# Hedgehog feed: keys and queries of a tile in one pair of banks, values in single banks, sums and turned features two tiles behind, maxima over both banks

## The chip, the cores and the metric

The kernel runs on one core of one Trainium2 chip. The metric is the device time of one execution in microseconds (us). Before the change it is 2536.88 us, the median of three runs (2536.19 to 2537.71).

The engines are named as in the profile: PE (TensorE, matmul; PEld is its weight load), DVE (VectorE), ACT (ScalarE), POOL (GpSimd) and SP (SyncE, which here issues DMAs). PSUM is the memory that PE writes to; this kernel uses it as three pairs of banks (pool `psS`, 1024 f32 a partition each) and two single banks (pool `ps1`, 512 f32 each).

## The reference

Four layers on 2048 tokens of width 512, 32 heads of width 16: softmax attention (A), Hedgehog linear attention (B), A, B. Each adds its output to x.

```python
x = x + _A_ref(_layernorm(x), A_wqkv, A_wo)
x = x + _B_ref(_layernorm(x), B_wqkv, B_w_phi, B_wo)
x = x + _A_ref(_layernorm(x), A_wqkv, A_wo)
x = x + _B_ref(_layernorm(x), B_wqkv, B_w_phi, B_wo)

# inside _B_ref, per head:
pq = q @ w_phi                      # the kernel folds w_phi into the weights of q and k
pk = k @ w_phi
phi_q = concat(softmax(pq), softmax(-pq))
phi_k = concat(softmax(pk), softmax(-pk))
kv, z = phi_k^T v, sum(phi_k)
o = (phi_q @ kv) / (phi_q @ z + 1e-6)
```

## The kernel before

The tokens are cut into 16 tiles of 128 and into four blocks `j` of four tiles. A layer of type A (`LayerA.attention`) walks 512 steps, one for each group of four heads, query block and key tile. In a step PE makes scores (L909), ACT takes two exponentials of 128x1024 (L912), and PE multiplies an earlier step's exponentials by the values (L923). Between these PE gets pieces of side work from a queue of generators (`pump`), by a credit per step. One kind of side work is `tail(j)` (L961): the last part of the output projection of block j (`o_block`, two halves of two tiles), the residual sum (L603), and the layer norm of that block for the next layer. `Norm.half` (L495) runs after each half: `stats` (mean, and an inverse root by three Newton steps on 128x2 numbers) and, after the first half, `scaled` for tiles 0 and 1. `Norm.steps` (L513) then turns the four tiles on PE (L476), splits each into two f16 parts (L484 or L486, and L489), and calls `scaled` for tiles 2 and 3.

Where these run depends on flags. In the attention `state["att"]` is true: `stats` uses DVE and leaves the bias `b` as None (L445 to L455), and `scaled`, finding no bias, uses DVE (L461). After the attention `att` is false: `stats` runs its Newton steps on POOL (L441 to L443) and makes `b`, and `scaled` uses ACT (L463). With `soon` the Newton steps go to DVE in either case, and a bias is made (L448). Tails 0 to 2 run inside the attention, tail 3 mostly behind it.

Behind each attention stands the feed of the next layer: `LayerB.feed(j)` for the 16 tiles. It is in a block in which PE, DVE, ACT and POOL each run their instructions in the order in which the program writes them. For a tile this order is, before the change:

- PE: 12 matmuls for the key features (`pk`), 12 for the query features (`pq`), eight transposes of the query features of the tile before (`turn`, into two single banks, with a copy by ACT each, L1207), 12 for the values (`pbv`), 24 small ones that add up keys by values of the tile before (`gather`, into `kvp`). `pk`, `pq` and `pbv` take a pair from `psS` each and use half of it; one of the three pairs is held by `kvp` through the whole feed.
- DVE and ACT: for the keys and then for the queries the largest and smallest feature of each head (L1155, L1156), two differences (L1158, L1159) and the exponential (L1160, `expo`); then the copy of the values (ACT, L1128).
- DVE: the sum of the keys' exponentials (L1166), its reciprocal (L1167), a factor (L1169); the low part of the values (L1123); then sum and reciprocal for the queries. POOL multiplies by the reciprocals (L1175), keys first.
- ACT copies the keys' features to f16 (L1181, `halves`), POOL makes their low part (L1182).
- `between(t)`: pieces of tail 3. In tiles 0 to 3 a part of the output projection each (with `half` after tiles 1 and 3), in tiles 5 to 8 one turned tile each (PE L476, ACT L486, DVE L489).

`psum1` hands out the two single banks in strict alternation when `att` is false; whoever gets one waits until its last user has released it. Tile 15 has its own branch: its key features are split between DVE and POOL, two turned tiles are left to `rest`, which then makes the heads.

Of the kernel before, what the change touches and what calls it, by code (L numbers as in the profile page):

```python
# [9 lines left out]
F32 = mybir.dt.float32  # L10
# [3 lines left out]
AF = mybir.ActivationFunctionType  # L14
ALU = mybir.AluOpType
AX = mybir.AxisListType

P = 128
S = 2048
D = 512  # L20
H = 32
DH = 16
NC4 = D // P
NJ = S // 512
NT = S // P
# [11 lines left out]
KS = 16384.0  # L37
# [13 lines left out]
def mha_hedgehog_stack(ctx, tc, x_in, a_wqkv, a_wo, b_wqkv, b_wphi, b_wo, out, shmin=SHMIN):  # L51
    nc = tc.nc
# [115 lines left out]
    con = {}  # L168
# [235 lines left out]
    class Norm:  # L404
        def __init__(self, xts, name):
            self.xts = xts
            self.xnT = big([P, 2, NC4, 512], F16, f"xnT{name}")
            self.xn, self.par = {}, {}

        def stats(self, t0, n, soon=False):  # L410
            run(self.stats_parts(t0, n, soon))
# [82 lines left out]

        def half(self, t2):  # L495

            self.stats(2 * t2, 2)
            if t2 == 0:
                self.scaled(0), self.scaled(1)

# [145 lines left out]
    class LayerA:  # L646
# [314 lines left out]
        def tail(self, j, ob):  # L961
            xts = []
            ln = Norm(xts, f"a{self.li}_{j}")
            yield from o_block(j, {3: ob}, self.wo, con["oA"], self.x_dst, self.x_dst, xts, ln.half, wide=False, cs=(3,))
            for _ in ln.steps():
                yield GAP
                self.cost = 3
            self.out.append(ln.xnT)
# [98 lines left out]
    class LayerB:  # L1067
# [3 lines left out]
        def begin(self):  # L1071
            self.wqk = stgp.tile([P, 2, 2, NC4, 512], F16, tag="stg", name="wbqk")
            nc.sync.dma_start(self.wqk, dBqk)
            self.wv = []
            for a in range(2):
                t = wp.tile([P, NC4, 512], F16, tag="w", name=f"wbv{a}")
                nc.sync.dma_start(t, dBv[a])
                self.wv.append(t)
            self.kvp = None
            self.latek = self.lateq = None  # L1080
            self.qT, self.obs = [], []

        def feed(self, j, xnT, between=lambda t: None):

            if self.kvp is None:
                self.kvp = psS.tile([P, 2, 512], F32, tag="S", name="kvp")
            qT = [big([P, 4, 512], F32, f"qT{j}_{i}") for i in range(2)]
            self.qT.append(qT)
            for t in range(4):
                tt = 4 * j + t  # L1090

                def project(dst, w, passes=(0, 1, 2)):
                    for i in passes:
                        a, b = PASSES[i]
                        for c in range(NC4):
                            nc.tensor.matmul(dst, xnT[:, a, c, t * P:(t + 1) * P], w(b, c),  # L1096
                                             start=(i == 0 and c == 0), stop=(i == 2 and c == NC4 - 1))

                vt = np_.tile([P, 2, H, 17], F16, tag="yn", name="vt", bufs=5)
                nc.gpsimd.memset(vt[:, 0, :, 16:17], 1.0)  # L1100
                nc.gpsimd.memset(vt[:, 1, :, 16:17], 0.0)
                bank = lambda name: psS.tile([P, 2, 512], F32, tag="S", name=name)[:, 0, :]
                last = tt == NT - 1
                pk = bank("pk")
                project(pk, lambda b, c: self.wqk[:, 1, b, c, :])
                if last:
                    f_k = self.expo(pk)
                    self.kvb = np_.tile([P, 8, 32], F32, tag="yn", name="kvb", bufs=5)
                    nc.gpsimd.memset(self.kvb, 0.0)
                else:  # L1110
                    pq = bank("pq")
                    project(pq, lambda b, c: self.wqk[:, 0, b, c, :])
                if self.lateq is not None and tt < NT - 2:
                    self.turn(*self.lateq)
                pv_ = bank("pbv")
                project(pv_, lambda b, c: self.wv[b][:, c, :])
                if self.latek is not None:
                    self.gather(*self.latek)
                if last:
                    pq = bank("pq")  # L1120
                    project(pq, lambda b, c: self.wqk[:, 0, b, c, :], (0, 1))
                pvh = pv_.rearrange("p (h d) -> p h d", d=DH)
                low = lambda: nc.vector.scalar_tensor_tensor(  # L1123
                    vt[:, 1, :, 0:16], pvh, 2.0 ** -8, vt[:, 0, :, 0:16], op0=ALU.mult, op1=ALU.subtract)
                if not last:
                    f_k = self.expo(pk)
                    f_q = self.expo(pq)
                nc.scalar.activation(vt[:, 0, :, 0:16], pvh, AF.Copy, scale=2.0 ** -8)  # L1128
                if last:
                    fk = self.share_split(f_k, low)  # L1130
                    self.turn(*self.todo)
                    self.gather(tt, fk, vt)
                    project(pq, lambda b, c: self.wqk[:, 0, b, c, :], (2,))
                    self.blocks()
                    self.todo = [self.lateq, (tt, self.expo(pq), qT)]
                    for q in self.todo:
                        self.share(q[1], 1.0)
                    return
                self.share(f_k, KS)
                low()  # L1140
                if tt == NT - 2:
                    self.todo = self.lateq
                    self.latek = (tt, self.halves(f_k), vt)
                else:
                    self.share(f_q, 1.0)
                    self.latek = (tt, self.halves(f_k), vt)
                self.lateq = (tt, f_q, qT)
                between(tt)

        def expo(self, ps):  # L1150

            pf = ps.rearrange("p (h f) -> p h f", f=DH)
            mx = sp.tile([P, H], F32, name="mx")
            mn = sp.tile([P, H], F32, name="mn")
            nc.vector.tensor_reduce(mx, pf, AX.X, ALU.max)  # L1155
            nc.vector.tensor_reduce(mn, pf, AX.X, ALU.min)  # L1156
            f = pp.tile([P, H, 2, DH], F32, tag="p", name="f")
            nc.vector.tensor_tensor(f[:, :, 0, :], pf, mx.unsqueeze(2).to_broadcast([P, H, DH]), ALU.subtract)  # L1158
            nc.vector.tensor_tensor(f[:, :, 1, :], mn.unsqueeze(2).to_broadcast([P, H, DH]), pf, ALU.subtract)  # L1159
            nc.scalar.activation(f, f, AF.Exp, scale=con["pB"])  # L1160
            return f

        def part_sums(self, f, r, factor):

            su = sp.tile([P, r.stop - r.start], F32, name="su", bufs=4)
            nc.vector.tensor_reduce(su, f[:, r, :], AX.X, ALU.add)  # L1166
            nc.vector.reciprocal(su, su)  # L1167
            if factor != 1.0:
# [3 lines left out]
        def share(self, f, factor):  # L1172

            f3 = f.rearrange("p h s f -> p (h s) f")
            nc.gpsimd.tensor_tensor(f3, f3, self.part_sums(f3, slice(0, 64), factor), ALU.mult)  # L1175

        def halves(self, f):

# [260 lines left out]
```

## Time and profile before

| what | value |
|---|---|
| median of three runs | 2536.88 us |
| the profiled execution: its time | 2541.1 us |
| the profiled execution: its span | 2539.3 us |
| TensorE clock granted, mean | 0.983 |
| DVE busy | 974.3 us (38%) |
| POOL busy | 383.6 us (15%) |

The span is the time from the first to the last instruction; the execution's own time is 1.8 us longer. The times in the profile count from the start of the span. The first attention ends at about 1037 us and its feed at about 1211 us; the second attention ends at about 2289 us and its feed at about 2462 us. An engine's busy time is the union of its instructions; idle time of an engine that nobody waits for costs nothing.

### The profile page before, as it was taken

What the parts mean: (1) busy time and instruction counts of PE and PEld (TensorE: products, weight loads), DVE (VectorE), ACT (ScalarE), POOL (GpSimd) and SP (SyncE); (2) the same over time, 40 slices, a digit from 0 to 9 for tenths busy, and PEclk for the clock granted to TensorE, in tenths of its full rate; (3) what the DMA queues carried; (4) which work ended last, traced back from release to release, by engine and by line L of the source; (5) the groups of instructions that cost most, each with busy time, mean ns of one, the idle gap of its engine ahead of it and who ended that gap; (6) DMA issues with size and microseconds to landing.
All of it is one profiled execution on the core that took longest, in us unless ns stands there. A gap on an engine that the chain in (4) does not pass through costs nothing.

```text
span 2539.3 us, 51475 instructions
## 1 busy us (share of the span) xinstructions
PE 2433.9 (96%) x21346; PEld 750.3 (30%) x21346; DVE 974.3 (38%) x1886; ACT 2174.0 (86%) x2431; POOL 383.6 (15%) x521
## 2 busy tenths in 40 slices
PE   5999999999999999999789999999999999998998
PEld 3322222222232222345343222222222222224543
DVE  6211211212133316899961122112122111368897
ACT  5799999999999999544438999999999999994543
POOL 2100000101000000356440010000010000004552
PEclk8999999999999999999899999999999999999999
DMA  5510230132033512100133003202300351110003
GB/s 183 89 18 6 45 50 1 20 52 70 1 80 86 205 49 84 51 17 18 67 98 59 12 6 51 40 1 45 66 1 9 69 141 43 67 67 26 9 18 110
DMA packets 109694, 135.34 MB, mean 53 GB/s; under 512 B 63641, under 2 KB 64905, under 8 KB 107273
## 3 DMA queue, kind: packets, MB, share of 16 engines
q1 hardware_dynamic: 108264, 128.39, 20.3%
q0 software_dynamic: 1184, 3.55, 0.6%
q8 instruction: 169, 2.77, 0.4%
q14 instruction: 77, 0.62, 0.1%
HBM read 60.06 MB, written 39.85 MB: 39 GB/s over the span
## 4 chain that ended last, share of the span: by engine, by line
PE 78%; DVE 12%; ACT 5%; issue 3%; POOL 2%; DMA 0%; SPq 0%; ACTq 0%; POOLq 0%; DVEq 0%
PE pv L923 37%; PE s L909 21%; PE pqk L615 6%; PE po L615 5%; ACT p L912 3%; DVE su L1166 2%; PE pbv L1096 1%; PE pk L1096 1%; PE pq L1096 1%; PE pst L476 1%; DVE f L1158 1%; DVE f L1159 1%; DVE yt L560 1%; DVE mx L1155 1%; POOL f L1175 1%
## 5 line engine op out<-in xcount | busy, mean ns | idle before, releaser
L912 ACT ACTIVATE p<-s 128x1024 f32<-128x1024 f32 x2048 | 1887.7, 1111 | 12.4 <-PE s L909 9.9
L923 PE MATMUL pv<-p,v 128*32 128x512 f32 x8192 | 1092.8, 605 | 2.6 <-DVE yt L533 1.6
L909 PE MATMUL s<-kq 49*128 49x512 f16 x3872 | 605.0, 382 | 12.3 <-DMA kq<-sh 4.1
L909 PEld LDWEIGHTS <-kq 49*128 49x128 f16 x3968 | 136.3, 94 | 628.9 <-issue 617.4
L923 PEld LDWEIGHTS pv<-p,v 128*32 128x32 f32 x8192 | 161.9, 108 | 398.4 <-issue 367.9
L717 POOL TENSOR_TENSOR sq<-stg 128x512 bf16<-128x512 f16 x48 | 69.9, 1457 | 1046.2 <-DVE stg L791 943.3
L533 DVE STREAM_TRANSPOSE yt<-pv 128x512 f32<-128x512 f32 x64 | 45.8, 716 | 451.9 <-PE pv L923 441.5
L790 DVE TENSOR_SCALAR tq<-pqk,c_qk 128x512 f32<-128x512 f32 x48 | 36.0, 749 | 444.9 <-PE pqk L615 427.6
L1175 POOL TENSOR_TENSOR f<-f,su 128x1024 f32<-128x1024 f32 x62 | 119.8, 1933 | 383.9 <-DVE su L1169 352.4
L1096 PEld LDWEIGHTS <-xnTa 128*128 128x128 f16 x1152 | 110.8, 99 | 151.2 <-DVE f L1159 23.6
L615 PEld LDWEIGHTS <-wA 128*32 128x32 f16 (+1 forms) x2496 | 86.3, 97 | 196.4 <-issue 169.8
L603 DVE SCALAR_TENSOR_TENSOR xt<-po,c_oA,xt 128x512 f32<-128x512 f32 x64 | 47.1, 736 | 234.5 <-PE po L615 234.5
L615 PE MATMUL pqk<-xnTb,wA 128*32 128x512 f16 (+1 forms) x1248 | 116.8, 379 | 2.2 <-ACT xnTb L486 2.2
L615 PE MATMUL pqk<-xnT,wA 128*32 128x512 f16 (+1 forms) x1224 | 110.9, 379 | 1.8 <-ACT xnT L486 1.5
L1096 PE MATMUL pbv<-wbv,xnTa 128*128 128x512 f16 x384 | 94.0, 397 | 19.0 <-DVE f L1159 19.0
L1160 ACT ACTIVATE f<-f,c_pB 128x1024 f32<-128x1024 f32 x64 | 72.7, 1148 | 45.3 <-DVE f L1159 45.2
L1181 ACT ACTIVATE fk<-f 128x1024 f16<-128x1024 f32 x30 | 31.7, 1057 | 72.8 <-POOL f L1175 72.8
L615 PE MATMUL po<-woA,ob 128*32 128x512 f16 x1152 | 92.4, 379 | 0.0
L1096 PE MATMUL pk<-wbqk,xnTa 128*128 128x512 f16 x384 | 88.5, 379 | 0.0
L1096 PE MATMUL pq<-wbqk,xnTa 128*128 128x512 f16 x384 | 88.4, 379 | 0.0
L1166 DVE TENSOR_REDUCE su<-f 128x64 f32<-128x1024 f32 x64 | 77.5, 1211 | 9.1 <-ACT f L1160 8.2
L615 PE MATMUL po<-wbo,obB 128*128 128x512 f16 x336 | 76.7, 388 | 0.6 <-POOL obB L553 0.6
(284 smaller groups left out, 1862.7 us busy)
## 6 DMA issues: line engine op xcount, KB each, us to landing
kq<-stg SPq DMA_DIRECT2D x168, 128.0 KB
xd<-xt SPq DMA_DIRECT2D x40, 512.0 KB
xt<-xd SPq DMA_DIRECT2D x40, 512.0 KB
v<-vyt SPq DMA_DIRECT2D x384, 16.0 KB
oD<-osp SPq DMA_DIRECT2D x24, 256.0 KB
ob<-oD SPq DMA_DIRECT2D x8, 768.0 KB
xt<-in_A_x_dram SPq DMA_DIRECT2D x8, 512.0 KB
wbqk<-dBqk SPq DMA_DIRECT2D x2, 2048.0 KB
```

The source lines that it names most:

```text
L533: nc.vector.transpose(yt.rearrange("p a b -> p (a b)"), ps)
L603: nc.vector.scalar_tensor_tensor(xt[:, u, :], ps, co, xt[:, u, :], op0=ALU.mult, op1=ALU.add)
L615: nc.tensor.matmul(ps[r, :], w[:, r], x, start=(n == 0), stop=(n == of - 1), skip_group_check=cols)
L717: nc.gpsimd.tensor_tensor(sq, hi, hi, ALU.mult)
L790: nc.vector.tensor_scalar(tq, ps, cqk, CLAMP, op0=ALU.mult, op1=ALU.min)
L909: nc.tensor.matmul(s[:, u, :], self.side(g, half, r, 0, kt * P, P), self.side(g, half, r, 1, j * 512, 512), start=True, stop=True)
L912: nc.scalar.activation(pt, s, AF.Exp, scale=0.25 / (QS * QS))
L923: nc.tensor.matmul(acc[32 * hh:32 * hh + 32, :], self.oct[o]["v"][:, r:r + 32], pt[:, hh % 2, :], start=(kt == 0), stop=(kt == NT - 1), sk ...
L1096: nc.tensor.matmul(dst, xnT[:, a, c, t * P:(t + 1) * P], w(b, c), start=(i == 0 and c == 0), stop=(i == 2 and c == NC4 - 1))
L1160: nc.scalar.activation(f, f, AF.Exp, scale=con["pB"])
L1166: nc.vector.tensor_reduce(su, f[:, r, :], AX.X, ALU.add)
L1175: nc.gpsimd.tensor_tensor(f3, f3, self.part_sums(f3, slice(0, 64), factor), ALU.mult)
```

## The change

In `feed` the keys' and the queries' features of a tile are two halves of one pair of banks (`both`); the values go to a single bank from `psum1`. `expo` takes `both` and finds the maxima, and then the minima, of one or two halves with one instruction each. The two sums are made first, then the low part of the values, then one reciprocal over all 128 sums and one factor over the keys' 64; `shared` multiplies on POOL. `halves` comes after `between(t)`. `turn` and `gather` are called for the tile two before (`lateq` and `latek` are queues now), and `gather` comes ahead of the values' matmuls. In the last tile the two tiles still queued are gathered around the values' matmuls. `tail` sets `soon` for its `Norm`, and `half` passes it on.

```diff
--- before.py
+++ after.py
@@ -405,7 +405,7 @@
         def __init__(self, xts, name):
             self.xts = xts
             self.xnT = big([P, 2, NC4, 512], F16, f"xnT{name}")
-            self.xn, self.par = {}, {}
+            self.xn, self.par, self.soon = {}, {}, False
 
         def stats(self, t0, n, soon=False):
             run(self.stats_parts(t0, n, soon))
@@ -494,7 +494,7 @@
 
         def half(self, t2):
 
-            self.stats(2 * t2, 2)
+            self.stats(2 * t2, 2, self.soon)
             if t2 == 0:
                 self.scaled(0), self.scaled(1)
 
@@ -961,6 +961,7 @@
         def tail(self, j, ob):
             xts = []
             ln = Norm(xts, f"a{self.li}_{j}")
+            ln.soon = True
             yield from o_block(j, {3: ob}, self.wo, con["oA"], self.x_dst, self.x_dst, xts, ln.half, wide=False, cs=(3,))
             for _ in ln.steps():
                 yield GAP
@@ -1077,7 +1078,7 @@
                 nc.sync.dma_start(t, dBv[a])
                 self.wv.append(t)
             self.kvp = None
-            self.latek = self.lateq = None
+            self.latek, self.lateq = deque(), deque()
             self.qT, self.obs = [], []
 
         def feed(self, j, xnT, between=lambda t: None):
@@ -1099,70 +1100,76 @@
                 vt = np_.tile([P, 2, H, 17], F16, tag="yn", name="vt", bufs=5)
                 nc.gpsimd.memset(vt[:, 0, :, 16:17], 1.0)
                 nc.gpsimd.memset(vt[:, 1, :, 16:17], 0.0)
-                bank = lambda name: psS.tile([P, 2, 512], F32, tag="S", name=name)[:, 0, :]
                 last = tt == NT - 1
-                pk = bank("pk")
+                both = psS.tile([P, 2, 512], F32, tag="S", name="pkq")
+                pk, pq = both[:, 0, :], both[:, 1, :]
                 project(pk, lambda b, c: self.wqk[:, 1, b, c, :])
                 if last:
-                    f_k = self.expo(pk)
+                    f_k, = self.expo(both, (0,))
                     self.kvb = np_.tile([P, 8, 32], F32, tag="yn", name="kvb", bufs=5)
                     nc.gpsimd.memset(self.kvb, 0.0)
                 else:
-                    pq = bank("pq")
                     project(pq, lambda b, c: self.wqk[:, 0, b, c, :])
-                if self.lateq is not None and tt < NT - 2:
-                    self.turn(*self.lateq)
-                pv_ = bank("pbv")
+                if len(self.lateq) > 1 and not last:
+                    self.turn(*self.lateq.popleft())
+                if len(self.latek) > 1:
+                    self.gather(*self.latek.popleft())
+                pv_ = psum1("pbv")
                 project(pv_, lambda b, c: self.wv[b][:, c, :])
-                if self.latek is not None:
-                    self.gather(*self.latek)
                 if last:
-                    pq = bank("pq")
+                    self.gather(*self.latek.popleft())
                     project(pq, lambda b, c: self.wqk[:, 0, b, c, :], (0, 1))
                 pvh = pv_.rearrange("p (h d) -> p h d", d=DH)
                 low = lambda: nc.vector.scalar_tensor_tensor(
                     vt[:, 1, :, 0:16], pvh, 2.0 ** -8, vt[:, 0, :, 0:16], op0=ALU.mult, op1=ALU.subtract)
                 if not last:
-                    f_k = self.expo(pk)
-                    f_q = self.expo(pq)
+                    f_k, f_q = self.expo(both, (0, 1))
                 nc.scalar.activation(vt[:, 0, :, 0:16], pvh, AF.Copy, scale=2.0 ** -8)
                 if last:
                     fk = self.share_split(f_k, low)
-                    self.turn(*self.todo)
+                    self.turn(*self.lateq.popleft())
                     self.gather(tt, fk, vt)
                     project(pq, lambda b, c: self.wqk[:, 0, b, c, :], (2,))
                     self.blocks()
-                    self.todo = [self.lateq, (tt, self.expo(pq), qT)]
+                    self.todo = [self.lateq.popleft(), (tt, self.expo(both, (1,))[0], qT)]
                     for q in self.todo:
                         self.share(q[1], 1.0)
                     return
-                self.share(f_k, KS)
+                su = sp.tile([P, 128], F32, name="su", bufs=2)
+                for i, f in enumerate((f_k, f_q)):
+                    nc.vector.tensor_reduce(su[:, 64 * i:64 * i + 64], f.rearrange("p h s f -> p (h s) f"), AX.X, ALU.add)
                 low()
-                if tt == NT - 2:
-                    self.todo = self.lateq
-                    self.latek = (tt, self.halves(f_k), vt)
-                else:
-                    self.share(f_q, 1.0)
-                    self.latek = (tt, self.halves(f_k), vt)
-                self.lateq = (tt, f_q, qT)
+                nc.vector.reciprocal(su, su)
+                nc.vector.tensor_scalar(su[:, 0:64], su[:, 0:64], KS, None, op0=ALU.mult)
+                self.shared(f_k, su[:, 0:64])
+                if tt < NT - 2:
+                    self.shared(f_q, su[:, 64:128])
                 between(tt)
-
-        def expo(self, ps):
-
-            pf = ps.rearrange("p (h f) -> p h f", f=DH)
-            mx = sp.tile([P, H], F32, name="mx")
-            mn = sp.tile([P, H], F32, name="mn")
+                self.latek.append((tt, self.halves(f_k), vt))
+                self.lateq.append((tt, f_q, qT))
+
+        def expo(self, both, which):
+
+            n = len(which)
+            pf = both[:, which[0]:which[0] + n, :].rearrange("p q (h f) -> p (q h) f", f=DH)
+            mx = sp.tile([P, 2 * H], F32, name="mx", bufs=2)[:, 0:n * H]
+            mn = sp.tile([P, 2 * H], F32, name="mn", bufs=2)[:, 0:n * H]
             nc.vector.tensor_reduce(mx, pf, AX.X, ALU.max)
             nc.vector.tensor_reduce(mn, pf, AX.X, ALU.min)
-            f = pp.tile([P, H, 2, DH], F32, tag="p", name="f")
-            nc.vector.tensor_tensor(f[:, :, 0, :], pf, mx.unsqueeze(2).to_broadcast([P, H, DH]), ALU.subtract)
-            nc.vector.tensor_tensor(f[:, :, 1, :], mn.unsqueeze(2).to_broadcast([P, H, DH]), pf, ALU.subtract)
-            nc.scalar.activation(f, f, AF.Exp, scale=con["pB"])
-            return f
+            fs = []
+            for i in range(n):
+                x = pf[:, i * H:(i + 1) * H, :]
+                wide = lambda t: t[:, i * H:(i + 1) * H].unsqueeze(2).to_broadcast([P, H, DH])
+                f = pp.tile([P, H, 2, DH], F32, tag="p", name="f")
+                nc.vector.tensor_tensor(f[:, :, 0, :], x, wide(mx), ALU.subtract)
+                nc.vector.tensor_tensor(f[:, :, 1, :], wide(mn), x, ALU.subtract)
+                nc.scalar.activation(f, f, AF.Exp, scale=con["pB"])
+                fs.append(f)
+            return fs
 
         def part_sums(self, f, r, factor):
 
-            su = sp.tile([P, r.stop - r.start], F32, name="su", bufs=4)
+            su = sp.tile([P, 128], F32, name="su", bufs=2)[:, 0:r.stop - r.start]
             nc.vector.tensor_reduce(su, f[:, r, :], AX.X, ALU.add)
             nc.vector.reciprocal(su, su)
             if factor != 1.0:
@@ -1173,6 +1180,10 @@
 
             f3 = f.rearrange("p h s f -> p (h s) f")
             nc.gpsimd.tensor_tensor(f3, f3, self.part_sums(f3, slice(0, 64), factor), ALU.mult)
+
+        def shared(self, f, su):
+            f3 = f.rearrange("p h s f -> p (h s) f")
+            nc.gpsimd.tensor_tensor(f3, f3, su.unsqueeze(2).to_broadcast([P, 64, DH]), ALU.mult)
 
         def halves(self, f):
```

## The prediction

> **What bounds the kernel now.** I read the page first, then busy time by stage (the windows view: from:to, length, then each engine's busy us).
>
> ```profile
> span 2539.3 us, 51475 instructions
> ```
> ```profile
> core 0: us, PE busy (x) PEld busy (x) DVE busy (x) ACT busy (x) POOL busy (x), PEclk, DMA share, GB/s
> ...
> 900.00:1036.00 136.00, 135.85 (x1242) 34.99 (x1240) 61.15 (x165) 135.17 (x147) 0.51 (x1) 1.00 0.19 67
> 1036.00:1114.00 78.00, 70.86 (x480) 35.84 (x472) 71.29 (x115) 33.37 (x43) 42.90 (x58) 0.96 0.08 27
> ```
>
> The attention (first row) fills PE and ACT; DVE is half idle. The first half of the feed (second row) is different: PE and DVE share it, neither full, ACT and POOL half used. The change touches both.
>
> Inside the attention, the timeline of ACT and the two lines that make the scaled tiles of a norm (L461 on DVE, L463 on ACT):
>
> ```profile
> 949.01 51.50 ACT L912 ACTIVATE p<-s 128x1024 f32<-128x1024 f32 x56
> ```
> ```profile
> L461 DVE TENSOR_SCALAR xn<-xt,mv,ly x24: 539/545/549, 965.3 to 2271.6; 128x512 f32<-128x512 f32 x24
> ```
> ```profile
> 1068.48 1.52 ACT L463 ACTIVATE xn<-xt,lb,ly 128x512 f32<-128x512 f32 x2 [7.17 <-POOL lb L453]
> 1069.90 1.06 ACT L1207 ACTIVATE qT<-pqt 128x512 f32<-128x512 f32 x2
> ```
>
> 56 exponentials follow each other in 51.50 us without a gap, 0.92 each: ACT has no room there.
>
> In the feed, tiles 5 to 8 run like this (timeline, one engine a fence):
>
> ```profile
> 1115.81 0.68 DVE L1159 TENSOR_TENSOR f<-mn,pq 128x512 f32<-128x512 f32 x1
> 1116.40 1.21 DVE L1166 TENSOR_REDUCE su<-f 128x64 f32<-128x1024 f32 x1
> 1117.65 0.55 DVE L1167 RECIPROCAL su<-su 128x64 f32<-128x64 f32 x1
> 1118.24 0.20 DVE L1169 TENSOR_SCALAR su<-su 128x64 f32<-128x64 f32 x1
> 1118.35 0.69 DVE L1123 SCALAR_TENSOR_TENSOR vt<-pbv,vt 128x512 f16<-128x512 f32 x1
> 1118.95 1.21 DVE L1166 TENSOR_REDUCE su<-f 128x64 f32<-128x1024 f32 x1
> 1120.19 0.55 DVE L1167 RECIPROCAL su<-su 128x64 f32<-128x64 f32 x1
> 1122.12 0.69 DVE L489 TENSOR_TENSOR xnTa<-pst,xnTa 128x512 f16<-128x512 f32 x1 [1.37 <-ACT xnTa L486]
> 1122.72 0.68 DVE L1155 TENSOR_REDUCE mx<-pk 128x32 f32<-128x512 f32 x1
> ```
> ```profile
> 1116.52 1.15 ACT L1160 ACTIVATE f<-f,c_pB 128x1024 f32<-128x1024 f32 x1 [1.24 <-DVE f L1159]
> ...
> 1120.54 1.06 ACT L1181 ACTIVATE fk<-f 128x1024 f16<-128x1024 f32 x1 [2.38 <-POOL f L1175]
> 1121.51 0.58 ACT L486 ACTIVATE xnTa<-pst 128x512 f16<-128x512 f32 x1
> 1121.98 0.80 ACT L463 ACTIVATE xn<-xt,lb,ly 128x512 f32<-128x512 f32 x1
> ```
> ```profile
> 1118.58 1.93 POOL L1175 TENSOR_TENSOR f<-f,su 128x1024 f32<-128x1024 f32 x1 [4.44 <-DVE su L1169]
> ```
>
> A loop shows: DVE's factor, POOL's product (1118.58), ACT's copy of the keys (1120.54), behind it in ACT's order the split of tail 3 (1121.51), which DVE awaits (idle 1.37) ahead of the next maxima. In tiles 10 to 14, with no piece of tail 3 in between, PE is the bound (chain of waits):
>
> ```profile
> 1157.30 2.59 PE pbv L1096 x12
> 1159.89 0.75 PE kvp L1213 x24
> 1160.64 2.59 PE pk L1096 x12
> 1163.23 2.59 PE pq L1096 x12
> 1165.82 0.87 PE pqt L1206 x8
> ```
>
> The sum is 9.39 us a tile, all PE. PE's starts cut the feed in three (timeline of PE; the first tile's `pk` and `pq`, then the `pk` of tiles 5, 10 and 15), and DVE goes on behind tile 15:
>
> ```profile
> 1037.20 0.59 PE L1096 MATMUL pk<-wbqk,xnTa 128*128 128x512 f16 x2
> ...
> 1040.78 2.75 PE L1096 MATMUL pq<-wbqk,xnTa 128*128 128x512 f16 x12
> 1097.32 2.75 PE L1096 MATMUL pk<-wbqk,xnTa 128*128 128x512 f16 x12
> 1150.81 2.75 PE L1096 MATMUL pk<-wbqk,xnTa 128*128 128x512 f16 x12
> 1197.32 2.75 PE L1096 MATMUL pk<-wbqk,xnTa 128*128 128x512 f16 x12
> ```
> ```profile
> 1200.12 0.69 DVE L1155 TENSOR_REDUCE mx<-pk 128x32 f32<-128x512 f32 x1 [1.06 <-PE pk L1096]
> ```
>
> Tiles 5 to 9 take 10.7 us each, 10 to 14 take 9.3.
>
> **Part 1: `soon` in the attention.** Tails 0 to 2 of both layers now have a bias, so `scaled` no longer takes DVE: the 24 L461 instructions become 24 on ACT. DVE loses what it has to spare; ACT gains work where it is full. Two L463 and the step to the next instruction took 1.42 to 1.52, 0.76 each: 24 x 0.76 = 18.2. Ends: 0.47 each (in the ACT fence below, the 512-wide L486 frees ACT that soon, 1121.51 to 1121.98), 11.3; 0.80 each (a whole L463, same fence), 19.2. About 1 is absorbed where ACT waits anyway. I take **+17**.
>
> **Part 2: the steady tile.** Let M be the start of the maxima over both halves. DVE's 512-wide instructions start 0.60 apart, a 1024-wide one takes 1.21 and frees DVE after 1.14. So: maxima and minima 2.28, four differences 2.40, M+4.7. The queries' exponential ends at M+5.9, the second sum runs from M+5.95, the low part from M+7.1, the reciprocal from M+7.7. Reciprocals by size:
>
> ```profile
> L1167 DVE RECIPROCAL su<-su x64: 509/553/554, 1047.7 to 2468.2; 128x64 f32<-128x64 f32 x64
> ```
> ```profile
> L563 DVE RECIPROCAL rec<-rec x32: 295/336/353, 1218.7 to 2517.8; 128x32 f32<-128x32 f32 x32
> ```
>
> 32 more numbers cost 0.22, 128 cost 0.99 (ends: 0.55 and 1.10). The factor ends at M+8.9. POOL starts 0.14 later, ends at M+11.0; ACT's copy of the keys frees ACT 0.97 later, M+12.0. Only then come, in ACT's order, the copies of the turned features, the first done at M+12.6. The single banks alternate and a tile takes two for `turn` and then one for the values, so **the values always get the bank of the first turned half**: PE's `pbv` of the next tile cannot start before M+12.6. Behind it on PE wait 2.59 of `pbv`, 0.42 of tail 3's turning (tiles 5 to 8), `pk` and `pq` with 2.59 + 2.75. The maxima of the tile after the next then start at M+20.6, or 21.0: **10.3 to 10.5 us a tile**. The wait on the pair of banks goes (pk's and pq's pair is free a tile earlier), and tail 3's split now stands ahead of the keys' copy, so the old loop goes too; this new one is late next. It beats the old 10.7 of tiles 5 to 9 a little, but not 9.39. DVE has some 9.4 of work in such a tile and fits in.
>
> **Part 3: the start.** The first maxima wait for `pq`: 1040.78 + 2.75 gives M0 = 1043.6, and DVE's work on tile 0 (9.0) and a residual of tail 3 (0.7) give M1 = 1053.3. Then the statistics of tail 3 run on DVE, behind tile 1. Before, POOL did them, and one tiny DVE instruction met a POOL product (DVE, then POOL):
>
> ```profile
> 1062.64 2.00 DVE L427 TENSOR_SCALAR ly<-lu 128x2 int32<-128x2 int32 x1
> ```
> ```profile
> 1062.49 2.13 POOL L1182 TENSOR_TENSOR fk<-f,fk 128x1024 f16<-128x1024 f32 x1
> ```
> ```profile
> 1031.58 0.17 DVE L427 TENSOR_SCALAR ly<-lu 128x2 int32<-128x2 int32 x1
> ...
> 1033.55 0.55 DVE L461 TENSOR_SCALAR xn<-xt,mv,ly 128x512 f32<-128x512 f32 x1
> ```
>
> It took 2.00 instead of 0.17 and ended 0.02 after POOL's. Now the whole statistic falls beside POOL's two products of its tile. I charge one such wait of 1.9 after tile 1 and one after tile 3, and 2.4 of tiny steps (2.0 in the last fence, L427 to L461, with the ends): M2 = 1053.3 + 9.0 + 0.6 (residual) + 1.5 (moments) + 1.9 + 2.4 = 1068.7. ACT's two `scaled` (1.5), the keys' copy and the first turned copy follow, `pbv` of tile 2 at 1071.9, M3 = 1080.5, the second statistic, M4 = 1095.9, `pk` of tile 5 at 1095.7 (1097.32 before). Without the two waits all later starts are 3.8 earlier.
>
> [...]
>
> **Part 4: the sum.** M5 = M4 + 9.0 = 1104.9; `pbv` of tile 5 waits until M4 + 12.6 = 1108.5 and `pk` of tile 6 starts at 1111.5. By the loop of part 2 tile 10 starts at 1153.1 (1150.81) and tile 15 at 1204.2 (1197.32). M14 = 1199.7, and DVE is done with tile 14 at M14 + 8.9 = 1208.6: 8.5 behind the row at 1200.12, because both maxima wait for `pq`. The last exponential then waits 0.5 behind the keys' copy. The extra gather and turn there lie beside DVE's chain, at nothing; uncovered they cost 0.75 + 0.87. So **+9.0 a feed, +18 for two**. Ends: +5 a feed without the waits on POOL, +12 with dearer reductions and a second wait each.
>
> In all 17 + 18 = **+35**: 2541.1 becomes 2576.1. The median lies 4.2 below the profiled run, so 2536.88 becomes **2572**. Its own range is 2553 to 2588.
>
> **Rivals.**
> - **Faster: `pbv` never waits.** If the first turned copy is done by M+11.0, where PE comes to `pbv` at 9.39 a tile, PE sets the pace. 15 tiles of 7.77, 13 of 0.87 + 0.75, pieces of tail 3 (4 x 0.65, 4 x 0.42) and 1.0 at the start make 143, against 1197.32 - 1037.20 = 160.1 (first and last `pk`; the 1.0 is what the first `pk` takes over 2.59); less 2.9 given back at tile 15 it is -14.2 a feed. With +17: 2526. For it: DVE and PE leave idle time. Against: 1.6 us must vanish from a chain of quoted rows in a fixed order. Chance 0.15.
> - **The attention absorbs the 24.** PE is as full there; if PE alone were the bound, part 1 is 0: 2555. Against: ACT's unbroken 51.50. Chance 0.12.
> - **ACT stands still for the statistics.** ACT's order in the attention is a planner's; a `scaled` put too early waits for DVE, and all exponentials behind it, for which PE waits. Six pairs at up to 2 us: 2584. Chance 0.13.
>
> **How the numbers follow.** Forecast 0.60. 0.2% (5 us) is about what a measurement can tell. Faster takes the first rival and 0.01: 0.16; same 0.05, from the low ends of parts 1 and 2 together; slower 0.79. The range 2550 to 2590 leaves out the first rival and the tails.
>
> **What would show it.** L461 on `xt` gone, 48 L463 on `xt`; gaps of 0.7 to 0.8 in the exponentials near 965 to 1036; `pbv` idle ahead, released by ACT's `qT`; `pk` starts 20.6 apart over two tiles in tiles 10 to 14; tiny DVE steps of about 2 us beside POOL; the maxima of tile 15 some 17 us later than 1200. If `pk` starts come 9.4 apart, part 2 is wrong; if exponentials keep 0.92 throughout, part 1 is.

## The result, and the profile after

The changed kernel takes **2585.34 us** (median of six runs, 2584.46 to 2586.12), the kernel before 2537.15 beside it. The ratio is **1.0189, 95% interval 1.0178 to 1.0200**: slower by 48.2 us. The forecast was 2572, the range 2550 to 2590. From the page of after, the span and two groups (the line's busy us and mean ns; then the idle time ahead of it and what ended most of it):

```profile
span 2583.8 us, 51414 instructions
...
L1097 PE MATMUL pbv<-wbv,xnTa 128*128 128x512 f16 x384 | 95.1, 401 | 31.8 <-ACT qT L1218 31.8
L463 ACT ACTIVATE xn<-xt,lb,ly 128x512 f32<-128x512 f32 x48 | 37.8, 816 | 54.6 <-POOL lb L453 36.2
```

The row of the page of before that answers to the first:

```profile
L1096 PE MATMUL pbv<-wbv,xnTa 128*128 128x512 f16 x384 | 94.0, 397 | 19.0 <-DVE f L1159 19.0
```

`pbv` now waits for ACT's turned features, 31.8 us in the two feeds, as forecast; before it waited 19.0 for DVE's release of a pair. And `scaled` is on ACT 48 times; the 36.2 us in which it waits for POOL lie in the layers of type B, which the change leaves as they were.

Where the time went is read from two stretches of each trace: the **attention**, from the end of the first exponential (L912) to the end of the last, and the **feed**, from the start of the first `pk` to the start of the last maxima (tile 15's queries). This table is used by all that follows; "span" is that of the profiled execution.

| kernel | attention 1, 2 | feed 1, 2 | span | median | ratio, 95% interval |
|---|---|---|---|---|---|
| before | 948.6, 945.1 | 173.6, 172.9 | 2539.3 | 2537.15 | 1 |
| after | 955.6, 951.9 | 189.6, 188.9 | 2583.8 | 2585.34 | 1.0189 (1.0178 to 1.0200) |
| e1_soon_last | 948.1, 944.5 | 189.6, 189.4 | 2570.2 | 2573.54 | 1.0145 (1.0128 to 1.0162) |
| e2_no_soon | 948.4, 943.9 | 187.7, 184.9 | 2562.6 | 2564.94 | 1.0110 (1.0093 to 1.0127) |
| e3_copy_later | 955.3, 953.1 | 179.6, 177.4 | 2561.9 | 2564.47 | 1.0107 (1.0091 to 1.0124) |
| e4_before_soon | 955.9, 951.8 | 179.3, 177.0 | 2563.4 | 2564.88 | 1.0106 (1.0089 to 1.0123) |
| e5_gather_last | 955.3, 954.5 | 188.5, 188.0 | 2584.9 | 2586.78 | 1.0196 (1.0179 to 1.0213) |
| e8_stats_first | 955.8, 953.2 | 184.4, 181.5 | 2574.9 | 2575.90 | 1.0149 (1.0133 to 1.0166) |
| e9_keep_busy | 955.5, 951.9 | 189.3, 187.0 | 2581.3 | 2583.13 | 1.0181 (1.0164 to 1.0198) |
| e10_before_copy | 948.1, 943.9 | 166.9, 165.8 | 2522.8 | 2525.16 | 0.9952 (0.9936 to 0.9969) |
| e11_single_max | 956.0, 953.1 | 190.4, 190.3 | 2587.9 | 2589.61 | 1.0201 (1.0184 to 1.0218) |
| e12_three_undone | 948.1, 945.1 | 169.8, 170.9 | 2531.1 | 2531.68 | 0.9974 (0.9963 to 0.9986) |
| e13_two_behind | 948.4, 945.1 | 176.8, 174.8 | 2542.6 | 2543.45 | 1.0018 (1.0009 to 1.0028) |
| e14_scaled_late | 948.9, 943.8 | 163.0, 162.2 | 2516.4 | 2517.41 | 0.9921 (0.9904 to 0.9937) |

From before to after the span grew by 44.5: 7.0 + 6.8 in the attentions, 16.0 + 16.0 in the feeds, and -1.3 elsewhere. (The medians differ by 48.2, because the profiled run of before lay some 4 us above its median.)

**The attention.** The timeline of ACT in after:

```profile
956.08 9.33 ACT L912 ACTIVATE p<-s 128x1024 f32<-128x1024 f32 x10
965.22 1.55 ACT L463 ACTIVATE xn<-xt,lb,ly 128x512 f32<-128x512 f32 x2
966.64 3.79 ACT L912 ACTIVATE p<-s 128x1024 f32<-128x1024 f32 x4
```

Two `scaled` stand in the row of exponentials. The next one starts at 966.64 instead of 965.22: 1.42 for two, 0.71 each.

**The loop.** Timeline of after, tiles 11 and 12, all engines:

```profile
1164.80 5.34 PE L1097 MATMUL pkq<-wbqk,xnTa 128*128 128x512 f16 x24
...
1170.18 1.23 DVE L1157 TENSOR_REDUCE mx<-pkq 128x64 f32<-128x1024 f32 x1 [1.88 <-PE pkq L1097]
...
1178.85 0.20 DVE L1143 TENSOR_SCALAR su<-su 128x64 f32<-128x64 f32 x1
1179.22 3.82 POOL L1186 TENSOR_TENSOR f<-f,su 128x1024 f32<-128x1024 f32 x2 [4.50 <-DVE su L1143]
...
1179.80 1.04 PE L1217 MATMUL pqt<-ident,f 128*128 128x128 f32 x8
...
1181.18 1.06 ACT L1192 ACTIVATE fk<-f 128x1024 f16<-128x1024 f32 x1 [4.59 <-POOL f L1186]
1182.15 1.07 ACT L1218 ACTIVATE qT<-pqt 128x512 f32<-128x512 f32 x2
...
1182.78 2.75 PE L1097 MATMUL pbv<-wbv,xnTa 128*128 128x512 f16 x12 [1.19 <-ACT qT L1218]
...
1185.37 4.91 PE L1097 MATMUL pkq<-wbqk,xnTa 128*128 128x512 f16 x22
```

The chain from the maxima at 1170.18 (M) can be followed row by row: factor done at M+8.87, keys' copy from M+11.00, turned copies from M+11.97, and `pbv` from M+12.60. The transposes that the turned copies read were done at 1180.84 (1179.80 + 1.04), 1.3 us before; the copies stand behind the keys' copy only because ACT runs in order. From 1164.80 to 1185.37 it is 20.57 for two tiles; 20.6 was forecast.

**The statistics.** DVE in after, behind tile 1 (the first two rows) and tile 3, then POOL behind tile 3:

```profile
1070.96 1.91 DVE L426 TENSOR_SCALAR lu<-mv 128x2 f32<-128x2 f32 x1
1072.91 0.17 DVE L427 TENSOR_SCALAR ly<-lu 128x2 int32<-128x2 int32 x1
...
1099.48 1.89 DVE L426 TENSOR_SCALAR lu<-mv 128x2 f32<-128x2 f32 x1
1101.41 2.36 DVE L427 TENSOR_SCALAR ly<-lu 128x2 int32<-128x2 int32 x1
1103.38 0.40 DVE L433 TENSOR_SCALAR lu<-lu 128x2 f32<-128x2 f32 x1
...
1105.64 1.22 DVE L1157 TENSOR_REDUCE mx<-pkq 128x64 f32<-128x1024 f32 x1
```
```profile
1097.53 3.83 POOL L1186 TENSOR_TENSOR f<-f,su 128x1024 f32<-128x1024 f32 x2 [6.35 <-DVE su L1143]
1101.31 2.13 POOL L1193 TENSOR_TENSOR fk<-f,fk 128x1024 f16<-128x1024 f32 x1
```

Behind tile 3 L426 ends with POOL's products (1101.37 and 1101.36); L427 starts as POOL's low part of the keys does, and the next step, L433, comes as that ends (1103.38 and 1103.44). One statistic has met two POOL instructions, where one was charged. Behind tile 1 it met only one: there ACT's two `scaled` stand ahead of the keys' copy that the low part needs, so that POOL starts it later.

**The granted clock.** PE in after in tile 2 (first row) and around tile 5, and windows of 1 us at tile 5 (PEclk is the third figure from the end):

```profile
1078.07 4.30 PE L1097 MATMUL pbv<-wbv,xnTa 128*128 128x512 f16 x12 [7.09 <-ACT qT L1218]
...
1108.86 0.60 PE L1217 MATMUL pqt<-ident,f 128*128 128x128 f32 x4
1113.47 1.12 PE L1217 MATMUL pqt<-ident,f 128*128 128x128 f32 x4 [4.01 <-DVE vt L1123]
...
1118.23 4.69 PE L1097 MATMUL pbv<-wbv,xnTa 128*128 128x512 f16 x12 [2.29 <-ACT qT L1218]
```
```profile
1111.00:1112.00 1.00, 0.00 (x0) 0.00 (x0) 1.00 (x2) 1.00 (x2) 0.00 (x0) 0.98 0.00 0
1112.00:1113.00 1.00, 0.00 (x0) 0.00 (x0) 1.00 (x2) 0.05 (x1) 0.00 (x0) 0.50 0.00 0
...
1121.00:1122.00 1.00, 1.00 (x3) 0.30 (x2) 1.00 (x1) 0.00 (x0) 0.00 (x0) 0.50 0.00 0
1122.00:1123.00 1.00, 1.00 (x7) 0.63 (x6) 0.08 (x1) 0.04 (x1) 0.00 (x0) 0.90 0.00 0
```

PE falls idle at 1109.46; from about 1112.0 to 1122.2 its granted clock is 0.50, and the 12 matmuls of `pbv` take 4.69 instead of 2.75. Tile 5 so pays 1.94 beside its wait. Tile 2 pays as well: its `pbv` comes after a wait of 7.09 and takes 4.30. In these windows the clock is either 1.00 or 0.50, and a mean of the two where it changes. Here the half came 2.5 us after PE fell idle and ended 4.0 us after `pbv` began (1118.23). In tile 2, where PE had been idle from 1070.98, it came after 3.4 us.

The kernel before already pays this price; PE in before, tile 2:

```profile
1067.08 4.38 PE L1096 MATMUL pbv<-wbv,xnTa 128*128 128x512 f16 x12 [2.75 <-DVE f L1159]
```

**The end of the feed.** Timeline of after, tile 15:

```profile
1220.07 0.68 DVE L1157 TENSOR_REDUCE mx<-pkq 128x32 f32<-128x512 f32 x1
...
1225.58 1.48 PE L1224 MATMUL kvp<-vt,fk 128*128 128x68 f16 x23 [2.00 <-POOL fk L1193]
...
1226.87 3.60 PE L1097 MATMUL pkq<-wbqk,xnTa 128*128 128x512 f16 x8
...
1233.74 0.69 DVE L1157 TENSOR_REDUCE mx<-pkq 128x32 f32<-128x512 f32 x1
```

PE's clock there (PEclk again third from the end):

```profile
1226.00:1234.00 8.00, 8.00 (x67) 4.76 (x64) 3.82 (x10) 2.50 (x5) 2.59 (x3) 0.66 0.00 0
```

and in before the last maxima:

```profile
1210.76 0.69 DVE L1155 TENSOR_REDUCE mx<-pq 128x32 f32<-128x512 f32 x1
```

From tile 15's first maxima to its last it is 13.67 now, 10.64 before (1200.12 to 1210.76). The gather of tile 14 waits 2.00 for POOL's low part (1.19 in before), and most of what stands behind it on PE runs at the low clock: eight matmuls of the queries take 3.60 (1.89 in before).

### The profile page after: what moved, and what is told of

Same layout as the page of the kernel before. It is cut to its first block, busy times and chain, and to the rows that moved or that the text cites. A ratio compares the mean times of both kernels' runs of the same rounds, so it can differ in the third digit from the quotient of the medians.

```text
span 2583.8 us, 51414 instructions
## 1 busy us (share of the span) xinstructions
PE 2440.3 (94%) x21346; PEld 757.1 (29%) x21346; DVE 972.6 (38%) x1832; ACT 2190.0 (85%) x2455; POOL 371.9 (14%) x465
## 4 chain that ended last, share of the span: by engine, by line
PE 75%; DVE 13%; ACT 6%; issue 3%; POOL 2%; DMA 0%; SPq 0%; ACTq 0%; POOLq 0%; DVEq 0%
PE pv L923 36%; PE s L909 20%; PE pqk L615 5%; ACT p L912 4%; PE po L615 4%; PE pkq L1097 3%; PE pbv L1097 2%; DVE su L1140 1%; DVE yt L560 1%; POOL f L1186 1%; DVE mx L1157 1%; DVE f L1165 1%; DVE f L1164 1%; PE pst L476 1%; DVE st L419 1%
## 5 line engine op out<-in xcount | busy, mean ns | idle before, releaser
L912 ACT ACTIVATE p<-s 128x1024 f32<-128x1024 f32 x2048 | 1888.6, 1112 | 10.2 <-PE s L909 7.8
L1097 PE MATMUL pkq<-wbqk,xnTa 128*128 128x512 f16 x768 | 175.5, 384 | 0.0
L1186 POOL TENSOR_TENSOR f<-f,su 128x1024 f32<-128x1024 f32 x58 | 111.0, 1934 | 415.8 <-DVE su L1143 394.0
L615 PEld LDWEIGHTS <-wA 128*32 128x32 f16 (+1 forms) x2496 | 86.3, 97 | 196.5 <-issue 169.8
L1097 PE MATMUL pbv<-wbv,xnTa 128*128 128x512 f16 x384 | 95.1, 401 | 31.8 <-ACT qT L1218 31.8
L463 ACT ACTIVATE xn<-xt,lb,ly 128x512 f32<-128x512 f32 x48 | 37.8, 816 | 54.6 <-POOL lb L453 36.2
```

What stands on the lines that cost most here:

```text
L463: nc.scalar.activation(xn, self.xts[t], AF.Identity, scale=y, bias=b)
L615: nc.tensor.matmul(ps[r, :], w[:, r], x, start=(n == 0), stop=(n == of - 1), skip_group_check=cols)
L912: nc.scalar.activation(pt, s, AF.Exp, scale=0.25 / (QS * QS))
L1186: nc.gpsimd.tensor_tensor(f3, f3, su.unsqueeze(2).to_broadcast([P, 64, DH]), ALU.mult)
```

## The experiments

Each is a small edit of after (e4, e10 and e14 of before).

**e1_soon_last: the attention's tails without `soon`.**

```diff
-            ln.soon = True
+            ln.soon = j == NJ - 1
```

> The changed kernel with soon set for tail 3 alone, so that tails 0 to 2 in the attention keep their scaled tiles on DVE. Theory (24 more instructions on a full ACT, 0.57 us each by the two traces): both attentions return to 948.6 and 945.1 us from first to last exponential, the feeds stay, 2585 becomes 2571 to 2572. Rival (the attention got longer for another reason, such as the bias or the planner's order): 2580 or more.

The attentions fall back to 948.1 and 944.5, the feeds stay; the span is 13.6 shorter, the median 11.8. So the 24 `scaled` on ACT cost the whole of the attentions' growth, and 24 x 0.71 = 17 shrank to 13.8, by 1.6 a layer.

**e2_no_soon: no `soon` at all, so that POOL makes tail 3's statistics.**

```diff
-            ln.soon = True
```

> The changed kernel without soon: the statistics of tail 3 go back to POOL, the scaled tiles of tails 0 to 2 back to DVE. Both theories give the attention its 13.7 us back. Theory (the statistics' place matters little, the wait of the values' matmuls on the turned copies carries the feed's loss): 2568 to 2576. Rival (the statistics on DVE carry the feed's loss, 4 to 6 us at each of two places in each feed): 2555 or less.

The attention comes back as in e1, the feeds give only 1.9 and 4.0. With POOL's statistics ACT's `scaled` waits (10.51 us behind tile 1, for L453), and the keys' copy behind it: the `pk` of tile 3 starts 23.4 us after that of tile 2, where after has 20.7. One loss is exchanged for another, and the time, 2564.94, lies between what the theory and the rival gave.

**e3_copy_later: the keys' copy behind the turned copies.** `halves` is called after the next tile's `turn` instead of at the end of the tile.

```diff
                     self.turn(*self.lateq.popleft())
+                if self.pend is not None and not last:
+                    self.keys()
...
-                self.latek.append((tt, self.halves(f_k), vt))
+                self.pend = tt, f_k, vt
...
+        def keys(self):
+            tt, f, vt = self.pend
+            self.latek.append((tt, self.halves(f), vt))
```

> The changed kernel with the copy of a tile's keys (and POOL's low part of it) written behind the next tile's turn, so that ACT makes the two turned copies ahead of it; nothing else is moved. Theory (the values' matmuls wait for the first turned copy, that for the keys' copy, that for POOL): pk starts of tiles 10 to 14 come 9.4 to 9.6 us apart instead of 10.3, tile 5 loses some 3 us of its wait, about 11 us a feed: 2560 to 2568. Rival (DVE's own work, or POOL's products, set the pace): tiles stay 10.3 apart and the time within 4 us of 2585.

The feeds lose 10.0 and 11.5. Timeline of e3:

```profile
1162.22 1.09 ACT L1225 ACTIVATE qT<-pqt 128x512 f32<-128x512 f32 x2 [3.41 <-PE pqt L1224]
...
1163.37 1.06 ACT L1199 ACTIVATE fk<-f 128x1024 f16<-128x1024 f32 x1
...
1165.79 5.34 PE L1097 MATMUL pkq<-wbqk,xnTa 128*128 128x512 f16 x24
...
1175.18 5.34 PE L1097 MATMUL pkq<-wbqk,xnTa 128*128 128x512 f16 x24
```

The turned copies now wait only for PE's transposes, `pbv` waits for nothing, and a tile takes 9.39. The loop is shown: with the keys' copy (and POOL's low part, which reads it) behind the turned copies, its wait is gone.

**e4_before_soon: `soon` alone, on the kernel before.**

```diff
+            ln.soon = True
...
-            self.stats(2 * t2, 2)
+            self.stats(2 * t2, 2, self.soon)
```

> The kernel before with soon for the tails and nothing else of the change. Theory (ACT in the attention +13.7; in the feed the statistics on DVE about as dear as on POOL, within 3 us a feed): 2545 to 2557. Rival (moving the statistics to DVE shortens the feed by what POOL took, 4 us at two places a feed): 2535 or less.

A miss for the theory: 2564.88. The attentions grow by 7.3 and 6.7 as in after, but the feeds by 5.7 and 4.1 too, where little was expected. The flag alone costs 24 us of span, over half of what the change costs.

**e5_gather_last: in tile 15, tile 14's gather behind the queries' matmuls and the turn.**

```diff
                 if last:
-                    self.gather(*self.latek.popleft())
                     project(pq, lambda b, c: self.wqk[:, 0, b, c, :], (0, 1))
...
                     self.turn(*self.lateq.popleft())
+                    self.gather(*self.latek.popleft())
                     self.gather(tt, fk, vt)
```

> The changed kernel with one call moved in the last tile: the gather of tile 14 comes behind the turn there, directly ahead of tile 15's own gather, instead of behind the values' matmuls. Theory (that gather waits for POOL's low part of tile 14 and holds the queries' projection and the turn behind it on PE, so that PE ends the feed late): the last maxima come 2 to 3 us earlier in each feed, 2579 to 2582. Rival (the chain DVE, ACT, POOL of tile 15 ends the feed anyway): within 1 us of 2585.

A miss: the feeds give 1.1 and 0.9, and the median is not lower (the intervals of e5 and after overlap). PE in e5:

```profile
1220.56 1.89 PE L1097 MATMUL pkq<-wbqk,xnTa 128*128 128x512 f16 x8 [0.80 <-DVE f L1165]
1225.91 1.11 PE L1217 MATMUL pqt<-ident,f 128*128 128x128 f32 x4 [3.03 <-DVE vt L1122]
1226.82 2.80 PE L1224 MATMUL kvp<-vt,fk 128*128 128x68 f16 x48
```

The queries' matmuls start 2.5 us behind tile 15's first maxima (1218.03 in e5) instead of 6.8, but the turn's second half then waits 3.03 for the bank of the values, and both gathers follow it. Taking the one wait away leaves the next; the end's 3 us are not settled further. The second attention was 2.6 us longer in this run, for which no run gives a reason, and that eats what the feeds gave.

**e8_stats_first: the statistics ahead of the reciprocal, before POOL has its products.**

```diff
                 low()
+                if tt < 4:
+                    between(tt)
                 nc.vector.reciprocal(su, su)
...
-                between(tt)
+                if tt >= 4:
+                    between(tt)
```

> The changed kernel with the piece of tail 3 of tiles 0 to 3 written ahead of the reciprocals, so that the statistics on DVE come before POOL gets a product to make. Theory (the first tiny steps wait for POOL's products): L426 and L427 fall from 1.9 and 2.4 us to 0.17 each, the maxima of tile 2 start 2 us earlier and those of tile 4 some 4 us earlier against their tile before, 4 to 6 us a feed: 2573 to 2578. Rival (these steps are slow for a reason on DVE itself): they keep their 1.9 us and the time stays within 4 of 2585.

The feeds lose 5.2 and 7.4. DVE in e8, behind tile 1:

```profile
1069.52 0.17 DVE L426 TENSOR_SCALAR lu<-mv 128x2 f32<-128x2 f32 x1
1069.72 0.17 DVE L427 TENSOR_SCALAR ly<-lu 128x2 int32<-128x2 int32 x1
```

0.17 each, where L426 took 1.91 there in after. Behind tile 3 of e8 the two steps take 0.17 each as well, where after has 1.89 and 2.36. The same work on the same engine, moved ahead of POOL's products (behind tile 1 of e8 their factor comes at 1072.75): the waits are POOL's doing.

**e9_keep_busy: the queries' matmuls of tiles 2 and 5 run three times, so that PE is idle for less long.** It is 48 matmuls a feed of repeated work.

```diff
-                    project(pq, lambda b, c: self.wqk[:, 0, b, c, :])
+                    for _ in range(3 if tt in (2, 5) else 1):
+                        project(pq, lambda b, c: self.wqk[:, 0, b, c, :])
```

> The changed kernel with the queries' projection of tiles 2 and 5 made three times over (the same numbers are written again), which fills time in which PE stands still there. It leaves nothing out. Theory (PE's clock is halved after such a stand, and that makes the values' projection of tile 5 take 4.7 us instead of 2.75): the granted clock stays at 1.0 near tiles 2 and 5, that projection takes 2.75, and each feed is about 2 us shorter in spite of the added work: 2579 to 2583. Rival (the half clock falls on waits only, or comes from something else): no gain, or the added 2 x 5.2 us show: 2585 or more.

Inconclusive in the time: -2.2 us, with overlapping intervals; the feeds give 0.3 and 1.9. PE in e9, and windows of 1 us:

```profile
1116.92 4.44 PE L1097 MATMUL pbv<-wbv,xnTa 128*128 128x512 f16 x12 [2.42 <-ACT qT L1219]
```
```profile
1114.00:1115.00 1.00, 0.50 (x17) 0.40 (x13) 1.00 (x2) 0.00 (x0) 1.00 (x1) 1.00 0.00 0
...
1117.00:1118.00 1.00, 1.00 (x4) 0.42 (x4) 0.00 (x0) 1.00 (x2) 1.00 (x2) 0.67 0.00 0
1118.00:1119.00 1.00, 1.00 (x3) 0.30 (x2) 0.00 (x0) 0.39 (x1) 1.00 (x1) 0.50 0.00 0
```

The half clock lasts 3.4 us instead of 10.2, but it falls on the same `pbv`, which still takes 4.44. PE still stands 2.42 ahead of it. In tile 2 `pbv` still waits 3.54 and takes 4.17. So the clock did not stay at 1.0 as expected, and filling part of this wait gained nothing that the time shows.

**e11_single_max: maxima and minima of keys and queries apart again.**

```diff
-                    f_k, f_q = self.expo(both, (0, 1))
+                    f_k, = self.expo(both, (0,))
+                    f_q, = self.expo(both, (1,))
```

> The changed kernel with the maxima, minima and differences made for the keys first and then for the queries, as before the change, from the same pair of banks; all else as changed. Theory (the maxima over both banks put DVE's start 2.6 us behind the keys' projection, and that closes the loop over the turned copies): pk starts of tiles 10 to 14 come 9.4 to 9.8 us apart, tile 15's first maxima again 2.8 us behind its pk, some 8 to 10 us a feed: 2565 to 2570. Rival (the copy that stands behind POOL's product binds whatever the maxima do): tiles stay at 10.3 and the time within 4 us of 2585.

A miss: 2589.61, not below after. Timeline of e11:

```profile
1165.47 5.34 PE L1097 MATMUL pkq<-wbqk,xnTa 128*128 128x512 f16 x24
1170.86 0.69 DVE L1158 TENSOR_REDUCE mx<-pkq 128x32 f32<-128x512 f32 x1 [1.84 <-PE pkq L1097]
```

The maxima over the keys alone still start only when the queries' matmuls are done (1165.47 + 5.34 = 1170.81). The two halves are one tile of the program, and its readers wait for the last write to either; in e5 the queries' matmuls wait 0.80 for reads of the keys' half in the same way. So it is the pairing, not the joint instruction, that puts M behind `pq`.

**e12_three_undone: e1, e3 and e8 together.**

> The changed kernel with three things undone together: soon for tail 3 alone, the keys' copy behind the next turn, the piece of tail 3 ahead of the reciprocals in tiles 0 to 3. Theory (these are separate costs; alone they gave 11.8, 20.9 and 9.4 us): the sum, 2541 to 2550. Rival (they count the same microseconds twice): 2555 or more.

2531.68: 53.7 below after, where the three alone gave 11.8, 20.9 and 9.4, 42.1 together. It is below the lower end of what was expected, and 0.26% below before. By the table's spans it is 52.7 against 44.4. Of these 8.3, 4.6 lie in feed 1, where the three alone gave 15.2 and e12 gives 19.8; in feed 2 it is 18.0 against 18.4, so that there the costs simply add up. One thing that differs in feed 1 is PE's clock: it is at half for 23.9 us in after and for 6.8 in e12, as in before. How much of the rest that explains was not measured by itself.

**e13_two_behind: after with e2, e3 and e11, so that the order two behind stands without `soon` and without the late copy.**

> What is left of the change when its dear parts are out: keys and queries in one pair of banks, values in single banks, sums and turned features two tiles behind, one reciprocal; but no soon, maxima of keys and queries apart, and the keys' copy behind the next turn. Theory (banks and distance are harmless, order and maxima were the cost): 2520 to 2532, at or below the kernel before. Rival (the distance of two tiles itself costs at the feed's end, or the single banks hold PE): 2540 or more.

A miss: 2543.45, 0.18% above before. Tiles 10 to 14 take 9.39 each, PE's pace, but with POOL's statistics the `pk` of tile 3 starts 23.1 after that of tile 2, and from tile 15's first maxima to its last it is 13.24, where before has 10.64. What is left of the change brings nothing over the old order.

**e10_before_copy: before, with `between(tt)` ahead of the keys' copy.** This is the one part of the change's order that the loop of before asks for.

```diff
+                between(tt)
                 self.latek = (tt, self.halves(f_k), vt)
                 self.lateq = (tt, f_q, qT)
-                between(tt)
```

> The kernel before with one order taken from the change: the piece of tail 3 comes ahead of the copy of the keys (and POOL's low part), nothing else. Theory (before, that copy, waiting for POOL, held tail 3's split and through it the next maxima in tiles 5 to 8): tiles 5 to 8 go from 11.1 to 9.8 us, some 5 to 7 us a feed: 2523 to 2528. Rival (DVE's own work is the bound in those tiles): within 3 us of 2537.

2525.16, faster than both kernels. Timeline of e10, tile 6:

```profile
1106.21 0.55 DVE L1166 RECIPROCAL su<-su 128x64 f32<-128x64 f32 x1
...
1106.68 0.63 DVE L489 TENSOR_TENSOR xnTa<-pst,xnTa 128x512 f16<-128x512 f32 x1
...
1107.22 0.68 DVE L1154 TENSOR_REDUCE mx<-pk 128x32 f32<-128x512 f32 x1
```

The idle 1.37 ahead of L489 is gone, since ACT's part of the split no longer stands behind the keys' copy; tiles 6 to 8 take 9.86 from `pk` to `pk`, where before took 10.79 to 11.11. Of feed 1's 6.7 us, 5.0 come from tiles 6 to 10. Another 2.6 come from tile 4, whose `pbv` in before waits 2.75 and takes 4.09 at the half clock, and here waits 0.67 and takes 2.76; tile 2 gives 1.2 back. One wait is left there, ACT's for tail 3's statistics on POOL:

```profile
1065.50 1.52 ACT L463 ACTIVATE xn<-xt,lb,ly 128x512 f32<-128x512 f32 x2 [8.81 <-POOL lb L453]
```

**e14_scaled_late: e10, and tail 3's `scaled` of tiles 0 and 1 made two tiles later**, when its statistics are long done.

```diff
-            if t2 == 0:
+            if t2 == 0 and not self.late:
                 self.scaled(0), self.scaled(1)
...
         def steps(self):
+            if self.late:
+                self.scaled(0), self.scaled(1)
...
+            ln.late = j == NJ - 1
```

> The kernel before with the order of e10 (the piece of tail 3 ahead of the keys' copy) and one more step moved: the scaled tiles 0 and 1 of tail 3 are made at tile 3 of the feed instead of tile 1, so that ACT no longer stands there until POOL has the statistics. Theory (an instruction that waits at the head of ACT's queue holds the exponentials and copies behind it, as in the loop of the changed kernel): the third tile's 16.1 us fall by about 4, 2514 to 2520. Rival (POOL's statistics, ahead of its low part of the keys, hold the gather anyway): within 3 us of e10, 2522 to 2528.

**2517.41, 0.79% below before** (interval 0.63% to 0.96%). The statistics still run on POOL, but nobody waits for them: from the `pk` of tile 2 (PE in e14, first row) to that of tile 3 (second) it is 12.23, with 16.09 in e10.

```profile
1057.74 2.76 PE L1099 MATMUL pk<-wbqk,xnTa 128*128 128x512 f16 x12
...
1069.97 2.77 PE L1099 MATMUL pk<-wbqk,xnTa 128*128 128x512 f16 x12
```

## Why the prediction was right, and what it missed

The sign, the two places and the two main mechanisms held; the time was 13 us too low. In the span +35 was forecast and +44.5 came: the attentions 3.2 less, the feeds 14.0 more, 1.3 less elsewhere. The other 4 us come from the medians: that of before lies 4.2 below its profiled run, that of after only 0.4. Some of the hit was luck. The feeds' +16.0 each lie beyond the upper end that the prediction gave for them (+12), and the ends of its terms add up to 2580 at most; the 2585 fell into the range by the margin around these ends, and the attentions' 3.2 us hide a part of the feeds' miss.

- **Part 1, right in kind, a little too dear.** 0.76 for a `scaled` was 0.71, and 3.2 of 17 were absorbed instead of about 1. e1 shows that nothing else lengthened the attention. The rival that the attention absorbs the 24 fell, and so did the one in which ACT stands still for the statistics there: ACT waits for them only twice, 0.29 and 0.75 us in the second attention, and the growth is that of the instructions, less what is absorbed.
- **Part 2, right to 0.1 us.** `pbv` at M+12.60 against M+12.6, two tiles in 20.57 against 20.6, and e3 shows that it was the copies' order. The rival that `pbv` never waits fell in after, and its 9.39 a tile is what e3 runs at. The prediction did not say that the pair of banks itself puts M behind `pq`; it put that down to maxima over both halves, and e11 shows that splitting them changes nothing.
- **Part 3, the terms mis-sized.** All counted from the first `pk`: the maxima of tile 2 come 0.7 us earlier than forecast, those of tile 4 at 61.5 (1105.64 - 1044.12) against 58.7 (1095.9 - 1037.20), 2.8 late. Two things lie between. `pbv` of tile 2 runs at the half clock, 4.30 instead of 2.75, and tile 3's maxima wait for the matmuls behind it: 1.6. And of "one such wait of 1.9 after tile 1 and one after tile 3" the second was two in a row: from L426 to the next maxima it is 6.16 behind tile 3 and 3.99 behind tile 1, 2.2 more. Then `pbv` of tile 5 runs at the half clock too, 1.9 more. Of the 7.0 a feed that were missing, the 2.8 and this make 4.7, and more of it is the clock than the second wait. The end "+12 with dearer reductions and a second wait each" was nearer than the +9 that was taken; it named the second wait, and the clock not at all.
- **Part 4, "at nothing" was wrong.** The extra gather and turn at tile 15 do not lie beside DVE's chain: PE waits ahead of the one, and runs the other slowly. From the first to the last maxima of tile 15 it is 13.67 instead of 10.64, 3.0 more, of which 0.5 was forecast. With the 4.7 this makes the 7.0 but for 0.2. What a better order would give there stays open: e5 took one wait away and met the next.

Waits that were counted right were thus followed by a cost that no row quoted in the prediction priced: behind them `pbv` ran at the half clock, 4.30 and 4.69 instead of 2.75 (after). The trace of before shows this cost, in the `pbv` of tile 2 (4.38) and of tile 4 (4.09).

## What to carry to other kernels

On an engine that runs in order, ask of each instruction that waits what stands ready behind it: moving one copy behind another on ACT was worth 21 us here (e3), and moving two `scaled` out from ahead of work that was ready another 8 (e10 to e14). The tiny DVE steps belonged ahead of POOL's products (0.17 us each in e8, 1.89 and 2.36 beside them in after), and work should leave an engine with slack only for another that has some (24 `scaled` on a full ACT cost 13.8 us of attention: after, e1). In this kernel the two halves of one PSUM tile wait for each other even where they are different banks (0.80 us in e5, 1.84 in e11), so a pair saves instructions at the price of overlap.

## What the runs showed of the hardware

- Two DVE steps of 128x2 numbers, 0.17 us each ahead of POOL's products (e8), took 1.89 and 2.36 us in a row beside two POOL instructions (after, behind tile 3). Each of them reads one tile (L426 `lu<-mv`, L427 `ly<-lu`).
- PE's granted clock takes two values in the traces of before and after, 1.00 and 0.50. The half did not come at a fixed time after PE fell idle: 3.4 us (idle from 1070.98) and 2.5 us (idle from 1109.46) in after, 2.8 us in e9 (idle from 1114.50), there when the work had begun again. In before PE stood for 2.93 us ahead of L476 at 1273.92, and the clock stayed at 1.00. Twelve matmuls of 128x512 that the half falls on took 4.30 and 4.69 us in after and 4.44 in e9, instead of 2.75. The stretches at half in the first feeds last 3.4 us (before and e9), 6.8 or 10.2 us (after).
